# Mamba-2 SSD and a SwiGLU feed-forward on one core: four products with decays moved to GpSimd, and a new order up to the first products of block 1

## The chip, the core and the metric

The kernel runs on one core of one Trainium2 chip. The core has five engines with an instruction queue each: TensorE (PE in the profile, with its weight loads shown as PEld), VectorE (DVE), ScalarE (ACT), GpSimd (POOL) and SyncE (SP), which here only issues DMAs. The metric is the time of one execution on the device in microseconds (us).

## The reference

A state-space layer (4 batches, 8 heads, 768 tokens, head size 32, state size 16), then an RMS norm and a SwiGLU feed-forward layer over the 3072 tokens (model size 256, hidden size 1536), all in float32:

```python
log_a = np.log(np.clip(a, 1e-06, 1.0))
for c in range(nc):                                   # chunks of the sequence
    cum = np.cumsum(la, axis=-1)
    L = np.exp(cum[:, :, :, None] - cum[:, :, None, :]) * causal
    CB = np.einsum('bhin,bhjn->bhij', Cc, Bc)
    y_intra = np.einsum('bhij,bhjd->bhid', CB * L, xc)
    decay_to_i = np.exp(cum)
    y_inter = np.einsum('bhin,bhnd->bhid', Cc, state) * decay_to_i[:, :, :, None]
    y[:, :, sl] = y_intra + y_inter
    decay_from_j = np.exp(cum[:, :, -1:] - cum)
    Bx = np.einsum('bhjn,bhjd->bhjnd', Bc, xc) * decay_from_j[:, :, :, None, None]
    state = np.exp(np.sum(la, axis=-1))[:, :, None, None] * state + np.sum(Bx, axis=2)
x = y.transpose(0, 2, 1, 3).reshape(B * S, H * D)
xn = x / np.sqrt(np.mean(x * x, axis=-1, keepdims=True) + 1e-06) * rms_g
g, val = xn @ w_gate, xn @ w_val
out = (g * (1.0 / (1.0 + np.exp(-g))) * val) @ w_out
```

## The kernel before

**The work.** Tokens go in six blocks of 512 (0 to 5). The state-space layer goes by chunks of 128 tokens in twelve pairs p (two pairs to a block); from pair 2 on each chunk is cut in halves of 64. For one pair: the decays L (`mask`, `sums`, `exp` in pairs 0 and 1; `spread`, `sub`, `ex` later), C and B times their decays (`scale`, L512, instruction L518: Cd = C times `to_i` in pairs 0 and 1 alone, Bd = B times `from_j` in all pairs), transposes of B and C (`turn`, `T`, `Tt`; of Cd: `last`, `Tl`), products CB (`g`, or `gg` for a pair at once, L576 and L583), L times CB (`L`, `L1`), the additions to the state (`A`) and the states (`S`, L670), and the outputs (`y`). ScalarE then takes y out (`yt`) and squares it (`sq`), PE means the squares (`ms`), ScalarE takes the roots (`rs`, a logarithm and an exponential), and VectorE normalizes (`xn`, L831).

**The weights** come in 18 pieces of integer words (`fetch.k`, a DMA that SyncE issues) and are rebuilt: `pow.k` on ScalarE, `man.k` and `wt.k` on VectorE (L216 and L219, L225). Pieces 0 to 11 are gate and value weights, 128 columns in pieces 0 and 1 and 256 in the following pairs of pieces; 12 to 17 are output weights.

**The feed-forward layer of block 0** is done by plain products for the first 768 hidden columns (`early.0`, `early.1`, `gate.2` to `gate.5`, each followed by `silu` and `hid`). All other products of gate and value weights use a Strassen-like scheme by groups j of 256 hidden columns: PE's `P.k.j` (L935; each is four 128x256 products), ScalarE's `take.k.j` (copies a bank, L941), VectorE's sums `C.c.j` (L947), `silug`/`silu` on ScalarE, and `hidg` on VectorE or `hidgp` on GpSimd (L960). It needs combinations of weights (`cw.j.k` on VectorE, `cwp.j.k` on GpSimd, L904) and of the normalized x (`tx.b.k`, `txp.b.k`, L912). Block 0's output products are `o.0` to `o.11` (L967).

**The order.** Everything is issued by one string of some 1600 steps, written out in the kernel, `block:step.arguments/bank`. Two tables (`first_kinds` for steps with the prefix `0:`, `kinds` for the rest) give each step its function, and the engine with it. Each engine, and SyncE's DMA queue, runs its own instructions in the order of the string, and waits at an instruction until what it reads is written and its buffer or PSUM bank is free. Of these buffers two matter below: c, the sums, has four (`bufs=4`); the banks of `P` have two for gate and two for val. So moving a step past steps of other engines changes nothing by itself; moving it past steps of its own engine changes what its engine does first.

Of the kernel before, what the change touches and what calls it, by code (L numbers as in the profile page):

```python
# [9 lines left out]
FP32 = mybir.dt.float32  # L10
# [5 lines left out]
ALU = mybir.AluOpType  # L16
# [4 lines left out]
def kernel(  # L21
# [42 lines left out]
    T = NB * S  # L64
# [447 lines left out]
    def scale(p):  # L512
        s = st[p]
        b, c0 = divmod(2 * p, NC)
        hs = slice(b * NH, (b + 1) * NH)
        for name, src, d in (("Cd", "C", to_i), ("Bd", "B", from_j))[0 if p < 2 else 1:]:
            s[name] = ssd.tile([P, 2, NH, N], FP32, tag=name, name=name)
            nc.vector.tensor_tensor(  # L518
                out=s[name], in0=s[src],
                in1=d[:, c0:c0 + 2, hs].unsqueeze(3).to_broadcast([P, 2, NH, N]), op=ALU.mult)  # L520
# [645 lines left out]
    def by_vector(out, in_, scale):  # L1166
# [10 lines left out]
        "scale": scale, "turn": turn,  # L1177
# [38 lines left out]
    def when(n, fn):  # L1216

        return lambda blk, *args: fn(blk + n, *args) if blk + n < NBLK else None

    def of_pair(n, fn):  # L1220
        return when(n, lambda b, p, *args: fn(2 * b + p, *args))

    def of_chunk(n, fn):
        return when(n, lambda b, g: fn(4 * b + g))
# [11 lines left out]
        "scale": of_pair(1, scale),  # L1236
# [12 lines left out]
        "ex": of_chunk(2, exponential), "scale2": of_pair(2, scale),  # L1249
        "table": when(2, lambda b: functions("silu")),  # L1250
# [208 lines left out]
```

## Time and profile before

| | |
|---|---|
| runs of the kernel before | 395.41, 395.79, 395.88 us; median 395.79 |
| the profiled execution | 395.41 us, its span 393.7 us |
| granted TensorE clock | 1.0 |
| HBM read / written | 22.64 / 3.74 MB |
| VectorE busy, 9–22 / 22–36 / 36–55 us | 12.25 / 13.60 / 18.48 us |
| VectorE busy, 55–70 / 70–80 / 80–95 us | 13.90 / 9.11 / 12.85 us |
| DMA engines busy, 22–36 / 36–55 / 55–70 us | 85% / 100% / 69% |

A row of an engine's timeline reads: start in us, duration in us, engine, line, operation, output and inputs by the program's names, shapes, number of instructions, and in square brackets the idle time before it with what ended that. A row of the waits reads: the waiting engine, its output and line, the engine and line that it waited for, the total in us, how often, and the longest. The first lines of the page give each engine's busy time and its share in 40 equal slices of the span (9.84 us each), in tenths.

### The profile page before, as it was taken

Reading aid. Unit: us, or ns where it says so; the run is one execution under the profiler, and the core shown is the slowest. Engines: PE = TensorE matmul, PEld = TensorE weight load, DVE = VectorE, ACT = ScalarE, POOL = GpSimd, SP = SyncE. Lnnn points to the kernel's source line nnn. Section 1 sums busy time; section 2 is a strip of 40 time slices with the busy share of each in tenths; the row PEclk is TensorE's granted clock in tenths of the full one; section 3 lists DMA queues with packets and bytes.
Section 4 is the critical chain, followed back from the end, with each engine's and each line's share of the span. In section 5 each row is a group of like instructions: output and inputs, shape, how many; then the busy total and the mean of one; then the engine's idle time right before and its main releaser. Section 6 shows DMA issues by size and latency. Waiting matters only on the chain.

```text
span 393.7 us, 9631 instructions
## 1 busy us (share of the span) xinstructions
PE 386.9 (98%) x3837; PEld 332.2 (84%) x3837; DVE 285.3 (72%) x594; ACT 234.1 (59%) x483; POOL 151.8 (39%) x170
## 2 busy tenths in 40 slices
PE   8999999999999999999999999999999999999996
PEld 5675478888888899888889888899888899988995
DVE  7999999997748967484897765676654587455574
ACT  3899889978599492447651544676345740555410
POOL 5022054454648378003563611466402155211271
PEclk9999999999999999999999999999999999999999
DMA  8988986682002538202423002000100000100001
GB/s 93 252 173 249 246 153 210 121 160 63 6 0 68 78 85 128 70 0 36 102 44 75 15 0 68 2 23 28 43 0 3 0 8 27 55 0 2 1 2 53
DMA packets 92533, 27.01 MB, mean 69 GB/s; under 512 B 77416, under 2 KB 86344, under 8 KB 92488
## 3 DMA queue, kind: packets, MB, share of 16 engines
q1 hardware_dynamic: 90408, 26.26, 29.8%
q8 instruction: 30, 0.49, 0.5%
q10 hardware_dynamic: 2080, 0.13, 0.4%
q14 instruction: 15, 0.12, 0.1%
HBM read 22.64 MB, written 3.74 MB: 67 GB/s over the span
## 4 chain that ended last, share of the span: by engine, by line
PE 81%; DVE 11%; issue 4%; ACT 3%; DVEq 0%; ACTq 0%
PE gate L935 27%; PE o L1056 21%; PE val L935 20%; PE o L967 4%; PE y L720 3%; PE g L583 1%; DVE wgv L225 1%; DVE m L219 1%; DVE m L216 1%; PE tp L533 1%; DVE hid L882 1%; PE g L576 1%; PE e L453 1%; PE y L648 1%; DVE S L672 1%
## 5 line engine op out<-in xcount | busy, mean ns | idle before, releaser
L947 DVE TENSOR_TENSOR c<-val,p 128x512 f32<-128x512 f32 x99 | 67.5, 687 | 40.3 <-PE val L935 28.3
L941 ACT COPY p<-gate 128x512 f32<-128x512 f32 x99 | 56.9, 584 | 58.0 <-PE gate L935 56.3
L960 POOL TENSOR_TENSOR hid<-c 128x256 f32<-128x256 f32 x41 | 34.0, 837 | 88.8 <-ACT c L197 82.6
L935 PE MATMUL gate<-tx,wgv 128*128 128x256 f32 x264 | 65.8, 382 | 0.0
L197 ACT ACTIVATE c<-c 128x256 f32<-128x256 f32 x99 | 39.3, 415 | 30.1 <-DVE c L947 29.6
L935 PEld LDWEIGHTS gate<-tx,wgv 128*128 128x128 f32 x264 | 49.0, 190 | 7.2 <-issue 0.3
L960 DVE TENSOR_TENSOR hid<-c 128x256 f32<-128x256 f32 x58 | 28.4, 498 | 17.0 <-ACT c L197 17.0
L1087 DVE TENSOR_TENSOR ob<-ob,o 128x128 f32<-128x128 f32 (+1 forms) x90 | 24.4, 299 | 20.7 <-PE o L1056 18.0
L1056 PE MATMUL o<-two,hid 128*128 128x128 f32 x280 | 36.2, 276 | 0.1
L1056 PEld LDWEIGHTS o<-two,hid 128*128 128x128 f32 x280 | 34.4, 192 | 1.1 <-issue 0.2
L935 PE MATMUL val<-tx,sw 128*128 128x256 f32 x132 | 34.0, 382 | 0.0
L935 PE MATMUL val<-xn,sw 128*128 128x256 f32 x132 | 33.7, 380 | 0.0
L935 PE MATMUL gate<-tx,sw 128*128 128x256 f32 x132 | 33.4, 381 | 0.0
L935 PE MATMUL gate<-xn,wgv 128*128 128x256 f32 x132 | 33.2, 381 | 0.2 <-DVE xn L831 0.2
L935 PE MATMUL val<-xn,wgv 128*128 128x256 f32 x132 | 33.3, 380 | 0.0
L486 POOL TENSOR_SCALAR_AFFINE_SELECT L<-L 64x512 f32<-64x512 f32 x32 | 23.0, 718 | 13.5 <-ACT L L197 10.9
L935 PEld LDWEIGHTS val<-tx,sw 128*128 128x128 f32 x132 | 24.7, 190 | 4.0 <-issue 0.4
L935 PEld LDWEIGHTS val<-xn,wgv 128*128 128x128 f32 x132 | 24.9, 190 | 3.4
L935 PEld LDWEIGHTS gate<-xn,wgv 128*128 128x128 f32 x132 | 24.4, 190 | 4.0 <-ACT e L197 0.6
L935 PEld LDWEIGHTS gate<-tx,sw 128*128 128x128 f32 x132 | 24.6, 190 | 3.4 <-issue 0.2
L197 ACT ACTIVATE u<-gate 128x256 f32<-128x256 f32 (+1 forms) x37 | 14.8, 402 | 21.2 <-PE gate L935 20.1
L935 PEld LDWEIGHTS val<-xn,sw 128*128 128x128 f32 x132 | 24.5, 190 | 3.2 <-issue 0.2
(199 smaller groups left out, 737.2 us busy)
## 6 DMA issues: line engine op xcount, KB each, us to landing
L<-rowd SPq DMA_DIRECT2D x32, 128.0 KB, 3.3
xr<-in_x_dram SPq DMA_DIRECT2D x24, 128.0 KB, 3.8
wr<-in_moe_w_out_dram SPq DMA_DIRECT2D x6, 512.0 KB, 3.6
out_dram<-ob SPq DMA_DIRECT2D x24, 128.0 KB, 1.7
wr<-in_moe_w_gate_dram SPq DMA_DIRECT2D x5, 512.0 KB, 6.3
wr<-in_moe_w_val_dram SPq DMA_DIRECT2D x5, 512.0 KB, 4.9
br<-in_B_dram SPq DMA_DIRECT2D x23, 64.0 KB, 2.9
cr<-in_C_dram SPq DMA_DIRECT2D x23, 64.0 KB, 2.9
```

The lines of the kernel that those rows point to most:

```text
L197: nc.scalar.activation(**operands)
L216: nc.vector.tensor_scalar(out=m, in0=hi, scalar1=0xFFFFF, scalar2=0x100000, op0=ALU.bitwise_and, op1=ALU.bitwise_or)
L219: nc.vector.scalar_tensor_tensor(out=f, in0=lo.bitcast(U32), scalar=2.0 ** -32, in1=m, op0=ALU.mult, op1=ALU.add)
L486: nc.gpsimd.affine_select(out=L[r], in_=L[r], pattern=[[0, L.shape[1]], [1, HC]], compare_op=ALU.is_ge, fill=0.0, base=0, channel_multipli ...
L720: nc.tensor.matmul(out=y[2 * k + u][rows, (2 * n + i) * HC:(2 * n + i + 1) * HC], start=(k, u, rows.start) not in opened, stop=True, skip_ ...
L935: nc.tensor.matmul(out=dst[:, half[w]], lhsT=lhsT, rhs=rhs, start=(k in (1, 2, 5) and w == 0), stop=True, skip_group_check=True)
L941: nc.scalar.copy(out=t, in_=Xs[j])
L947: nc.vector.tensor_tensor(out=t, in0=Zs[j], in1=a, op=ALU.add)
L960: engine.tensor_tensor(out=hid[:, 2 * j + c // 10 - 1, c % 10 - 1], in0=u, in1=src[:, half[1]], op=ALU.mult)
L967: nc.tensor.matmul(out=o, lhsT=hid[:, f, k // 2, (k % 2) * P:(k % 2 + 1) * P], rhs=wo[:, f], start=opens, stop=(f == NF - 1), skip_group_c ...
L1056: nc.tensor.matmul(out=Os[blk, b][:, place * P:(place + 1) * P], lhsT=hidden_or_sum(u)[:, g], rhs=rhs, start=(blk, b) not in opened, stop= ...
L1087: nc.vector.tensor_tensor(out=o, in0=o, in1=src, op=ALU.add if what[0] == "+" else ALU.subtract)
```

## The change

`scale` does one product a call (k = 0 for Cd, 1 for Bd) and takes the engine as an argument; a new step `scalep` calls it with GpSimd. The steps `0:scale.1` and `0:scale.0`, two VectorE products each, become `0:scalep.1.0`, `0:scalep.1.1`, `0:scalep.0.0` and `0:scalep.0.1` on GpSimd. Of pair 5 the product moves to GpSimd as well. (`scale2p` is defined and not used in the new stretch.)

Of the string, the part from `0:fetch.7` to `1:P.6.0` is in a new order. In it some further steps change their engine. From VectorE to GpSimd go `cw.0.1`, `cw.1.2`, `cw.3.1`, `cw.4.0`, `tx.1.0`, `tx.1.3`, `1:cw.2.0` and `cw.1.1`; from GpSimd to VectorE go `cwp.1.0`, `cwp.4.3`, `cwp.5.3` and `hidgp.11.3`, `hidgp.22.4`, `hidgp.12.3`. Among the other moves: `fetch.7` to behind `dT.2`; `pow.11` from ahead of `P.1.3` to behind `P.7.3`; `P.4.5` from behind `o.1` to ahead of it; `silug.22.4`, `silug.22.3`, `silug.12.3` and `silug.21.4` to ahead of `take.7.5`; `hidgp.11.5` to behind the GpSimd steps `txp.1.0`, `txp.1.1`, `1:cwp.2.0` and `cwp.0.1`; `man.17` to behind `1:C.11.1`. The lists of products and of DMAs are the same.

```diff
@@ -509,15 +509,15 @@
         subtract(g)
         exponential(g)
 
-    def scale(p):
+    def scale(p, k=1, engine=nc.vector):
         s = st[p]
         b, c0 = divmod(2 * p, NC)
         hs = slice(b * NH, (b + 1) * NH)
-        for name, src, d in (("Cd", "C", to_i), ("Bd", "B", from_j))[0 if p < 2 else 1:]:
-            s[name] = ssd.tile([P, 2, NH, N], FP32, tag=name, name=name)
-            nc.vector.tensor_tensor(
-                out=s[name], in0=s[src],
-                in1=d[:, c0:c0 + 2, hs].unsqueeze(3).to_broadcast([P, 2, NH, N]), op=ALU.mult)
+        name, src, d = (("Cd", "C", to_i), ("Bd", "B", from_j))[k]
+        s[name] = ssd.tile([P, 2, NH, N], FP32, tag=name, name=name)
+        engine.tensor_tensor(
+            out=s[name], in0=s[src],
+            in1=d[:, c0:c0 + 2, hs].unsqueeze(3).to_broadcast([P, 2, NH, N]), op=ALU.mult)
 
     def transposed(p):
         s = st[p]
@@ -1174,7 +1174,7 @@
         "r": sums_of_logs, "parts": three_parts,
         "d": other_sums, "dx": other_decays,
         "c": chunk_sums, "cx": chunk_decays, "cc": chunk_column,
-        "scale": scale, "turn": turn,
+        "scale": scale, "scalep": lambda p, k=1: scale(p, k, pl), "turn": turn,
         "T": lambda p: turned(p, ac.copy if p else dv.tensor_copy),
         "Tt": lambda p, t: turned_of(p, by_scalar, t), "Tb": turned_of_both,
         "dT": spread_decays, "Td": turned_decayed,
@@ -1233,7 +1233,7 @@
         "turn": of_pair(1, turn), "T": of_pair(1, lambda p: turned(p, ac.copy)),
         "Tt": of_pair(1, lambda p, t: turned_of(p, by_scalar, t)),
         "dT": of_pair(1, spread_decays), "Td": of_pair(1, turned_decayed),
-        "scale": of_pair(1, scale),
+        "scale": of_pair(1, scale), "scalep": of_pair(1, lambda p: scale(p, 1, pl)),
         "g": when(1, lambda b: products_of_block(b, pair_of_banks("g", 2))),
         "L": when(1, decayed_block), "L1": when(1, decayed_block),
         "A": of_pair(1, additions), "S": of_pair(1, states),
@@ -1247,6 +1247,7 @@
         "bc": of_pair(2, load), "x": of_pair(2, load_x), "spread": of_chunk(2, spread), "sub": of_chunk(2, subtract),
         "subp": of_chunk(2, lambda g: subtract(g, nc.gpsimd)),
         "ex": of_chunk(2, exponential), "scale2": of_pair(2, scale),
+        "scale2p": of_pair(2, lambda p: scale(p, 1, pl)),
         "table": when(2, lambda b: functions("silu")),
         "exps": when(1, lambda b: functions("exp")),
     }
@@ -1256,37 +1257,37 @@
         0:part 0:hmask 0:upto 0:mid 0:mids 0:part2 0:aT 0:mask.1.1/2 0:la0 0:log4.0.4 0:upto2 0:r.0
         0:fetch.2 0:head 0:sel 0:middles 0:after2 0:fetch.3 0:log4.4.2 0:log4.6.2 0:bc.3 0:tmask
         0:parts.0 0:log 0:c*2 0:cx 0:mask.0.1/1 0:turn.0 0:Tb.0 0:T.0 0:d 0:dx 0:sums.0.1 0:sums.0.0
-        0:exp.0.1 0:never16 1:exps 0:exp.0.0 0:turn.1 0:scale.1 0:last.1 0:cc 0:scale.0 0:T.1 0:mean
-        0:g.0.1/1 0:Tt.1.0 0:g.0.0/0 0:Tt.1.1 0:L.0.1 0:L.0.0 0:sums.1.1 0:exp.1.1 0:row.1
-        0:rowout.1 0:man.0 0:bc.2 0:mask.1.0/1 0:sums.1.0 0:rowe.1 0:g.1.1/0 0:L.1.1 0:Tl.1
-        0:g.1.0/2 0:exp.1.0 0:L.1.0 0:fetch.4 0:last.0 0:Tl.0 0:fetch.7 0:dT.2 0:tok 0:tokout 0:A.1
-        0:A.0 0:S.0 0:S.1 0:pow.0 0:wt.0 0:y.0/1 0:sq.0 0:pow.1 0:y.1/2 0:sq.1 0:row.0 0:yt.0
-        0:man.1 0:wt.1 0:mask.3/1 0:rowe.0 0:yt.1 0:ydone.1 0:r.1 0:man.3 0:scale.3 0:eps
-        0:early.0.0/0 0:early.0.1 0:rowout.0 0:ms.0 0:parts.1 0:pow.3 0:pow.2 0:wt.3 0:rs.0
-        0:mask.2/2 0:scale.2 0:man.2 0:wt.2 0:sums.3 0:sums.2 0:exp.3 0:turn.2 0:T.2 0:Tt.2.0 0:xn.0
-        0:turn.3 0:norm.0 0:T.3 0:Tt.3.1 0:Tt.2.1 0:fetch.5 0:Tt.3.0 0:exp.2 0:Td.2 0:early.1.0/1
-        0:early.1.1 0:dT.3 0:man.4 0:table.1 0:x.2 0:norm.1 0:man.5 0:Td.3 0:silu.0 0:hid.0 0:pow.4
-        0:gate.2/0 0:txp.0.0 0:cw.0.0 0:gg.2/1 0:L.2.0 0:wt.4 0:man.7 0:pow.5 0:wt.5 0:L1.2.2
-        0:fetch.8 0:fetch.9 0:silu.2 0:hid.2 0:man.8 0:pow.8 0:wt.8 0:L1.2.3 0:gate.3/2 0:pow.7
-        0:gate.4/1 0:fetch.6 0:man.6 0:A.2 0:txp.0.1 0:silu.3 0:x.3 0:table.0 0:hid.3 0:pow.6
-        0:gate.5/0 0:tx.0.2 1:dT.0 1:table 0:txp.0.3 0:fetch.11 0:wt.7 0:man.9 0:fetch.10 0:S.2
-        0:silu.4 0:pow.9 0:fetch.12 0:hid.4 0:bc.5 0:wt.6 0:cwp.3.0 0:wt.9 0:silu.5 0:hid.5 0:man.11
-        0:cw.3.1 0:cw.3.2 0:cw.4.0 0:fetch.13 0:silu.1 0:y.2/2 0:S.3 0:x.5 0:cwp.4.1 0:ydone.0
-        0:switch.1 0:P.2.3 0:bc.4 0:x.4 0:switch.0 0:pow.11 0:P.1.3 0:P.1.4 0:take.1.3 0:C.11.3
-        0:P.2.4 0:P.6.3 0:yt.2 0:sq.2 0:gg.3/2 0:take.1.4 0:silug.11.3 0:C.11.4 0:L.3.0 0:take.6.3
-        0:cwp.3.3 0:P.5.3 1:spread.0 0:cwp.1.0 0:P.7.3 0:silug.11.4 0:P.6.4 0:take.7.3 0:P.5.4
-        0:P.4.3 0:hidgp.11.3 1:dT.1 0:wt.11 0:L1.3.2 0:scale.5 0:L1.3.3 0:cwp.4.2 0:cwp.4.3
-        0:take.6.4 0:C.22.3 0:P.3.3 0:man.10 0:scale.4 0:pow.10 0:wt.10 0:silug.21.3 0:cwp.5.0
-        0:cwp.5.1 0:hidg.11.4 0:P.7.4 0:take.7.4 0:y.3/2 0:C.12.3 0:hidg.21.3 0:fetch.15 1:S.0 1:S.1
-        0:P.1.5 0:P.2.5 0:pow.12 0:P.4.4 0:take.1.5 0:C.11.5 0:cw.1.2 0:P.6.5 0:C.22.4 0:fetch.14
-        0:sq.3 0:cwp.5.2 0:yt.3 0:spread.10 1:spread.1 0:man.12 0:take.6.5 0:ms.1 0:P.5.5
-        0:spread.11 0:rs.1 1:turn.1 0:wt.12 0:silug.22.3 0:hidgp.22.3 0:hid.1 0:cwp.5.3 0:P.7.5
-        0:o.0/2 0:P.3.4 0:take.7.5 0:man.15 0:silug.12.3 0:cw.1.1 0:hidgp.12.3 0:silug.21.4 0:man.13
-        0:o.1 0:P.4.5 0:C.22.5 0:hidg.21.4 0:pow.13 0:wt.13 0:P.3.5 0:C.12.4 0:silug.22.4
-        0:hidgp.22.4 0:man.14 0:silug.21.5 0:silug.22.5 0:silug.11.5 0:C.12.5 0:pow.14 0:hidg.21.5
-        0:fetch.17 0:pow.15 0:o.2 0:cw.0.1 0:rb.1 0:o.3 0:xn.1 1:P.1.0 0:silug.12.5 0:wt.14
-        0:hidgp.11.5 0:man.17 1:bc.0 1:take.1.0 1:P.1.1 0:tx.1.0 1:P.2.1 1:T.1 0:txp.1.1 0:o.4
-        0:tx.1.2 1:take.1.1 1:P.6.1 0:pow.17 1:cw.2.0 0:hidgp.22.5 0:tx.1.3 1:C.11.1 1:silu.11.1
+        0:exp.0.1 0:never16 1:exps 0:exp.0.0 0:turn.1 0:scalep.1.0 0:scalep.1.1 0:last.1 0:cc
+        0:scalep.0.0 0:scalep.0.1 0:T.1 0:mean 0:g.0.1/1 0:Tt.1.0 0:g.0.0/0 0:Tt.1.1 0:L.0.1 0:L.0.0
+        0:sums.1.1 0:exp.1.1 0:row.1 0:rowout.1 0:man.0 0:bc.2 0:mask.1.0/1 0:sums.1.0 0:rowe.1
+        0:g.1.1/0 0:L.1.1 0:Tl.1 0:g.1.0/2 0:exp.1.0 0:L.1.0 0:fetch.4 0:last.0 0:Tl.0 0:dT.2 0:tok
+        0:tokout 0:A.1 0:A.0 0:S.0 0:S.1 0:pow.0 0:fetch.7 0:wt.0 0:y.0/1 0:sq.0 0:pow.1 0:y.1/2
+        0:sq.1 0:row.0 0:yt.0 0:man.1 0:wt.1 0:mask.3/1 0:rowe.0 0:yt.1 0:ydone.1 0:r.1 0:man.3
+        0:scale.3 0:eps 0:early.0.0/0 0:early.0.1 0:rowout.0 0:ms.0 0:parts.1 0:pow.3 0:pow.2 0:wt.3
+        0:rs.0 0:mask.2/2 0:scale.2 0:man.2 0:wt.2 0:sums.3 0:sums.2 0:exp.3 0:turn.2 0:T.2 0:Tt.2.0
+        0:xn.0 0:turn.3 0:norm.0 0:T.3 0:Tt.3.1 0:Tt.2.1 0:fetch.5 0:Tt.3.0 0:exp.2 0:Td.2
+        0:early.1.0/1 0:early.1.1 0:dT.3 0:man.4 0:table.1 0:x.2 0:norm.1 0:man.5 0:Td.3 0:silu.0
+        0:hid.0 0:pow.4 0:txp.0.0 0:txp.0.1 0:silu.1 0:wt.4 0:fetch.6 0:ydone.0 0:gate.3/2 0:gg.2/1
+        0:pow.5 0:cw.1.0 0:L.2.0 0:silu.3 0:fetch.11 0:L1.2.3 0:fetch.9 0:pow.6 0:L1.2.2 0:man.6
+        0:wt.5 0:hid.3 0:man.7 0:cwp.1.1 0:gate.2/0 0:A.2 0:silu.2 0:hid.2 0:gate.4/1 0:pow.7
+        0:fetch.8 0:S.2 0:wt.6 0:wt.7 0:gate.5/0 0:x.3 0:pow.9 0:man.8 0:silu.4 0:hid.4 0:pow.8
+        0:man.9 0:wt.9 0:cwp.3.0 0:silu.5 0:y.2/2 0:cw.3.2 0:hid.5 0:wt.8 0:cwp.3.1 0:cwp.4.0
+        0:switch.1 0:P.2.3 0:switch.0 0:tx.0.2 0:S.3 0:bc.4 0:man.11 0:yt.2 0:P.1.3 0:take.1.3
+        0:fetch.10 0:P.1.4 0:C.11.3 0:sq.2 0:P.2.4 0:scale.4 0:take.1.4 0:C.11.4 0:txp.0.3 0:P.6.3
+        0:gg.3/2 0:L1.3.2 0:P.5.3 0:take.6.3 0:P.7.3 0:pow.11 0:cwp.4.1 0:silug.11.3 0:cwp.3.3
+        0:P.5.4 0:L1.3.3 0:hid.1 0:L.3.0 0:P.6.4 0:bc.5 0:x.4 0:take.7.3 0:C.22.3 0:man.10 0:pow.10
+        0:cwp.4.2 0:P.4.3 0:silug.21.3 0:wt.11 0:hidg.21.3 0:wt.10 0:scalep.5 0:x.5 0:hidg.11.3
+        0:P.3.3 0:C.12.3 0:y.3/2 0:cwp.5.0 0:P.1.5 1:S.0 0:take.6.4 0:P.7.4 0:fetch.12 0:pow.12
+        0:fetch.13 0:P.2.5 0:silug.11.4 0:take.1.5 0:spread.10 0:fetch.17 0:take.7.4 0:cwp.5.1
+        0:P.6.5 0:P.4.4 0:fetch.14 1:S.1 0:sq.3 0:C.22.4 0:yt.3 0:man.12 0:take.6.5 0:fetch.15
+        0:cw.4.3 0:cwp.5.2 0:spread.11 1:turn.1 0:ms.1 0:P.7.5 0:hidg.11.4 0:rs.1 0:silug.22.4
+        0:C.11.5 0:cw.0.0 0:wt.12 0:silug.22.3 0:hidgp.22.3 0:P.3.4 0:P.5.5 0:silug.12.3 0:man.14
+        0:o.0/2 0:silug.21.4 0:take.7.5 0:C.22.5 0:hidg.21.4 0:man.13 0:P.4.5 0:o.1 0:pow.13
+        0:cw.5.3 0:wt.13 0:man.15 0:hidg.22.4 0:P.3.5 0:o.2 0:silug.21.5 0:hidg.21.5 0:o.3 1:table
+        0:pow.14 1:dT.0 0:wt.14 0:rb.1 0:cwp.1.2 0:xn.1 0:silug.22.5 0:C.12.4 0:hidgp.22.5 0:txp.1.0
+        1:spread.0 0:txp.1.1 0:hidg.12.3 0:silug.11.5 0:pow.15 1:P.1.1 1:take.1.1 0:C.12.5 1:cwp.2.0
+        0:tx.1.2 1:P.2.1 1:spread.1 1:C.11.1 0:cwp.0.1 0:silug.12.5 1:P.1.0 0:pow.17 1:P.6.1
+        0:table.0 0:o.4 1:dT.1 1:take.1.0 0:hidgp.11.5 1:bc.0 0:man.17 0:txp.1.3 1:T.1 1:silu.11.1
         1:P.6.0 1:sub.0 1:P.2.0 0:wt.15 0:wt.17 1:turn.0 1:C.11.0 0:cwp.0.2 1:Tt.1.0 1:hid.11.1
         1:take.6.0 1:P.7.0 1:take.7.0 1:take.6.1 1:silu.11.0 1:P.5.1 1:P.5.0 1:P.4.0 1:C.22.0
         0:cwp.0.3 0:fetch.16 1:silu.21.0 0:spread.9 1:P.7.1 1:P.3.0 1:cwp.2.2 1:hid.21.0 0:ydone.3
```

## The prediction

> **What bounds the kernel now.** I read the page first, then what TensorE (PE) waits for, then each engine's timeline where the steps differ (about 9.5 to 92 us).
>
> ```profile
> PE 386.9 (98%) x3837; PEld 332.2 (84%) x3837; DVE 285.3 (72%) x594; ACT 234.1 (59%) x483; POOL 151.8 (39%) x170
> ...
> PE   8999999999999999999999999999999999999996
> ...
> DVE  7999999997748967484897765676654587455574
> ```
>
> PE is busy in nearly every slice, VectorE (DVE) only until about 95 us. The page's first two parts say that time is PE's work plus the few places where PE has nothing to do. The change leaves PE's list of products as it was and only moves them. So it can gain no more than PE's idle places inside the reordered stretch, and it loses whatever new ones it makes. What PE waits for, over the whole span:
>
> ```profile
> PE idle L322 <- DVE warm L348: 1.1, 1, 1.1
> PE o L1056 <- DVE ob L1087: 0.9, 2, 0.5
> PE y L689 <- DVE S L670: 0.5, 1, 0.5
> PE g L583 <- ACT sq L197: 0.5, 1, 0.5
> PE gate L935 <- DVE xn L831: 0.2, 1, 0.2
> ```
>
> Only the last three lie after 9.5 us and before the old order resumes. Measured from start to start they are a little longer. Eight 128x256 products take 1.73 us (two groups of PE's timeline start at 88.25 and 89.98), 0.216 each; P.6.3 begins at 53.54, so gg.3 could begin at 54.40 and begins at 55.08: 0.68 us lost. o.2 and o.3 begin at 76.14, 16 products end at 79.60, block 1 begins at 79.97: 0.37 lost. **The ceiling of the gain is thus 0.68 + 0.37 = 1.05 us**; the wait for S.0 at 18.40 hangs on a chain that the first edit does not shorten (next paragraph).
>
> **The four steps on GpSimd.** On VectorE the products with the decays stand so:
>
> ```profile
> 9.50 0.43 DVE L518 TENSOR_TENSOR Cd<-cr,d_sb 128x256 f32<-128x256 f32 x1
> 9.84 0.42 DVE L518 TENSOR_TENSOR Bd<-br,d_sb 128x256 f32<-128x256 f32 x1
> ...
> 11.90 2.36 DVE L622 TENSOR_TENSOR L<-g,L 128x1024 f32<-128x1024 f32 x2 [0.33 <-PE g L576]
> ```
>
> Four of them free 4 x 0.34 = 1.36 us of VectorE (start to start), worth nothing: VectorE then already waits 0.33 us for PE's g, so it only waits longer. What can be lost is the other end: PE's transposes of Cd (last.1, 10.34) now wait for GpSimd. It is free from 9.03 (its 128x416 product starts at 7.97 and takes 1.06) and starts when d_sb is there, at 9.50. No row shows this product on GpSimd; a 128x256 product of two SBUF operands takes 0.73 alone (30.85) and up to 1.25 (85.23). Cd is ready at 10.23 to 10.75, the two transposes issue in 0.22, and g.0.1 starts at 10.65 whatever happens, since it waits for the exponential that ends at 10.54. So: nothing (with 0.73) to +0.4 us. I take 0: beside these steps VectorE runs a reduction and a memset, not work like that beside the 1.25 row. The Trainium skill (GPSIMD Engine Reference, "Elementwise — side-by-side cycle accounting") puts an elementwise product on GpSimd at 1.96 times VectorE's; that would be an estimated 0.83 us here, against 0.73 in the row, and 0 to the sum either way. Pair 1's Bd and pair 0's two end by about 12.6 (three more at 0.78) and are first read at 15.40 and 16.30: hidden, with 2.8 us to spare. Pair 5's product, which also goes to GpSimd, stands behind six others there, ends near 59.5 and is read at 62: hidden. Of the other steps that change engine between VectorE and GpSimd (combinations of weights and of x, three hidden products), VectorE is rid of seven in all; they count below where something waits for them.
>
> **The new order, 33 to 60 us.** fetch.7 goes behind dT.2 in SyncE's queue; its weights are first used 10 us after they land, and dT.3, moved back some 0.4 us, lands at 35.4 instead of 35.0, before its user at 35.97. Later x.5 waits for y.2 (about 50 us) and holds fetch.12 to fetch.15 behind it; fetch.12 then lands near 56 and is read at 61. Nothing here. VectorE's row of steps before S.3 loses man.11 (1.07, start to start), cw.3.1 and cw.4.0 (0.33 each), so S.3 starts near 51.1 instead of 52.78. ScalarE's yt.2 and sq.2 follow (2.2 us from S.3 to the end of sq.2 in the old rows: 52.78 to 55.02), and gg.3 finds its bank free at about 54.4: **-0.5 us** (0 if cwp.3.0 and cwp.3.1 slow man.8, -0.68 at best).
>
> **60 to 80 us.** ScalarE now does pow.11 (2.2) after take.6.3 instead of at 50.10, so it has no idle time left; sq.3 starts near 65.3 (65.69 before), and turn.1, which now waits for yt.3 with P.7.4 and P.4.4 already behind PE, takes back **+0.2 us** (0 to 0.75). rs.1 starts near 67.75 (68.14 before). After its two table loads of 1.28 the order puts four silu products (about 0.34 each) ahead of take.7.5, where one stood, so take.7.5 ends 5.2 us after rs.1 starts, at 73.0 (72.34 before); and P.4.5, which waits for it, now comes straight after o.0, with o.1 (1.73) no longer in front. PE is there 0.3 ahead of the old 72.69, at 72.4: **+0.65 us** (0 to 1.1). From 73.05 PE does P.4.5, o.1, P.3.5, o.2 and o.3 (0.86 + 1.73 + 0.86 + 3.46) until 79.96. VectorE does C.22.5, hidg.21.4, man.13, cw.5.3, wt.13, man.15, hidg.22.4, hidg.21.5 and wt.14 (0.60 + 0.33 + 1.07 + 0.33 + 0.62 + 1.07 + 0.33 + 0.33 + 0.62 = 5.3, from the rows' starts) until 78.3, so the first half of xn.1 (0.70) is there by 79.1 and the old wait for it goes: **-0.37 us** (0 if VectorE loses 0.9 on the way).
>
> **80 to 92 us, the step that decides.** GpSimd gets txp.1.0, cwp.2.0 and cwp.0.1 ahead of hidgp.11.5, and txp.1.3 behind it; C.11.1 on VectorE waits for hidgp.11.5 (its buffer), and behind C.11.1 stand man.17 (which ran before it), sub.0, wt.15, wt.17 and C.11.0, for which PE's P.5.0 waits. The rows there:
>
> ```profile
> 82.76 0.78 POOL L912 TENSOR_TENSOR tx<-xn,tx 128x256 f32<-128x256 f32 x1 [5.41 <-DVE tx L912]
> 83.49 0.91 POOL L960 TENSOR_TENSOR hid<-c 128x256 f32<-128x256 f32 x1
> 84.36 0.91 POOL L904 TENSOR_TENSOR wgv<-wgv 128x256 f32<-128x256 f32 x1
> 85.23 1.25 POOL L904 TENSOR_TENSOR sw<-wgv,sw 128x256 f32<-128x256 f32 x1
> ...
> 88.70 1.29 POOL L499 TENSOR_TENSOR L<-L,tok 128x512 f32<-128x512 f32 x1
> ```
>
> ```profile
> 82.86 0.95 DVE L904 TENSOR_TENSOR sw<-wgv 128x256 f32<-128x256 f32 x1
> ...
> 84.61 0.68 DVE L947 TENSOR_TENSOR c<-val,p 128x512 f32<-128x512 f32 x1
> 85.21 0.68 DVE L499 TENSOR_TENSOR L<-L,tok 128x512 f32<-128x512 f32 x1
> 85.81 2.35 DVE L225 SCALAR_TENSOR_TENSOR wo<-m,e 128x512 f32<-128x512 f32 x2
> 88.08 0.68 DVE L947 TENSOR_TENSOR c<-val,p 128x512 f32<-128x512 f32 x1
> ```
>
> The six GpSimd products from 82.76 to 88.70 take 0.99 us each from start to start. Five of them (txp.1.0, txp.1.1, cwp.2.0, cwp.0.1, hidgp.11.5) after xn.1's first half end at 84.1 if that ends at 79.1, at 84.8 if it ends at 79.78 as in the old rows; I take the later, since GpSimd also blocks xn.1 itself (last rival); C.11.1 starts at 84.9. From C.11.1 to C.11.0 the rows give 84.61 to 88.08 = 3.47; man.17 adds 1.07 (81.12 to 82.19); C.11.0 itself takes 0.68. Ready at 90.1. PE is at P.5.0 at 89.11 less 0.02 (the sum so far): a stall of about **+1.1 us**. Bounds: 0.70 per product (3.5 for five, the spacing of GpSimd alone at 55.10 to 56.48) and xn.1 0.7 earlier make C.11.0 ready at 88.0 and cost nothing; man.17 beside GpSimd (+0.41, L219 at 1.10 against 0.69) makes 1.5. I take 1.1 since the spacing of 0.99 is from this very stretch. Behind it the order is the old one and PE has no slack to give the time back.
>
> **Sum.** 0 - 0.5 + 0.2 + 0.65 - 0.37 + 1.1 = +1.1. The profiled execution took 395.41 us (span 393.7 and 1.7 around it), so 396.5 for one like it; the median of the three runs is 395.79, 0.38 higher, so **396.9** against that.
>
> **Rivals.**
> *No change (395.8).* The gain at gg.3 and the new wait at P.4.5 cancel (-0.02, with xn.1) and GpSimd runs at its uncontended 0.70, so C.11.0 is in time. For it: each step moved is hidden by about half a microsecond. Against: the 0.99 spacing.
> *Faster (394.7).* The wait for sq.2 and that for xn.1 both go and nothing comes back: -1.05, the ceiling. It needs take.7.5 to end by 72.0 (72.69 - 0.68), so rs.1 to begin by 66.8 instead of 68.14, and C.11.1 to start by 82.8 (89.11 - 1.05 - 3.47 - 1.07 - 0.68). Against: ScalarE has no idle time left before rs.1.
> *Every pair alternates (398.0).* A VectorE instruction with both inputs in SBUF shows 0.95 beside GpSimd against 0.42 alone, 1.22 against 0.69 (the second of the L225 pair). If man.8 (+0.7: 0.29 and 0.41) beside cwp.3.0 and cwp.3.1 pays it too, the gain at gg.3 is gone, S.1 and yt.3 come 0.75 late, and C.11.0 costs 1.45: +2.2. The Trainium skill (SBUF — State Buffer, "Who interferes with whom") speaks for this rival, and against the change as a whole: the pair of ports is a lock, and a VectorE instruction with two SBUF inputs and a GpSimd instruction that reads SBUF block each other entirely. By that rule, the rows at 82.86 and 85.81 agree.
> *The change not doing what it says* is out: the program has the five L518 products on GpSimd.
>
> **Chances.** Forecast 0.45, no change 0.30, faster 0.15, every pair 0.10. Some 0.2% (0.8 us) is what a measurement of this kernel can tell. The forecast's own range runs from +0.3 to +1.9, so a sixth of it falls within 0.2%; a little of the faster case does too, and a little of the middle falls out to either side: faster 0.16, same 0.34, slower 0.50. The range for 8 in 10 goes from the ceiling of the gain, 394.7, to the lock case with 0.4 for a late Cd, 398.4.
>
> **What would show it.** In the profile after: last.1 at 10.34 to 10.5 and g.0.1 at 10.65 (right) or near 11 (0.4 lost); no PE wait for sq before gg.3; a PE wait for ScalarE's p at L935 near 72.5; VectorE idle before the first C of block 1 near 82 to 84 with GpSimd as its releaser; and PE waiting 0.7 to 1.5 us for C.11.0 near 89. If PE's list of waits shows none of the last two, the forecast is wrong and the time is 395.8 or less; if it shows over 2 us in other places, a step that I called hidden was not.

## The result

The changed kernel takes 398.08 us (median of seven runs, 396.99 to 401.57) against 395.79 (seven runs, 395.41 to 396.13): 1.0077 times the kernel before, 95% interval 1.0049 to 1.0105. By the medians that is 2.3 us more, by the ratio 3.0. Forecast were 396.9, 1.1 more. Single executions whose granted TensorE clock was 0.991 to 0.996 instead of 0.999 to 1.0 took 397.6 to 401.6 us, whatever the kernel; two of these seven (400.96 and 401.57) and one of the control's six below (401.21) are such, and without those two the median is 397.86, 2.1 more. The profiled execution took 399.11 us, 1.0 above the median; its span is 397.4 against 393.7.

The first part of the page and the list of PE's waits, after:

```profile
PE 387.8 (98%) x3837; PEld 332.2 (84%) x3837; DVE 284.1 (71%) x587; ACT 233.8 (59%) x483; POOL 156.3 (39%) x177
```

```profile
PE val L935 <- DVE c L947: 1.8, 1, 1.8
PE g L583 <- DVE T L557: 1.2, 1, 1.2
...
PE gate L935 <- ACT p L941: 0.4, 2, 0.2
```

VectorE does seven instructions less and GpSimd seven more, PE's list is as long as before. Of the three waits of before inside the reordered stretch, two are gone (gg.3 for sq, block 1 for xn). Two that were not there are larger than both together: P.5.0 (val) waits 1.8 us for a C of VectorE, and gg.2 (g) waits 1.2 us for VectorE's product with the decays, T. The third line is P.6.3 and P.4.5, which wait for ScalarE's copies.

The first of the two, in VectorE's timeline (columns as before: start, duration, engine, line, operation, tiles, and the idle time ahead of it):

```profile
85.60 0.69 DVE L947 TENSOR_TENSOR c<-val,p 128x512 f32<-128x512 f32 x1 [2.02 <-POOL hid L960]
86.21 1.02 DVE L216 TENSOR_SCALAR m<-wr 128x512 int32<-128x512 int32 x1
87.27 1.10 DVE L219 SCALAR_TENSOR_TENSOR m<-wr,m 128x512 f32<-128x512 uint32 x1
88.29 1.21 DVE L499 TENSOR_TENSOR L<-L,tok 128x512 f32<-128x512 f32 x1
89.42 2.66 DVE L225 SCALAR_TENSOR_TENSOR wo<-m,e 128x512 f32<-128x512 f32 x2
92.01 0.68 DVE L947 TENSOR_TENSOR c<-val,p 128x512 f32<-128x512 f32 x1
```

and in GpSimd's, the instructions that ran beside it:

```profile
84.83 0.73 POOL L960 TENSOR_TENSOR hid<-c 128x256 f32<-128x256 f32 x1
85.52 0.74 POOL L912 TENSOR_TENSOR tx<-xn,tx 128x256 f32<-128x256 f32 x1
86.20 0.74 POOL L904 TENSOR_TENSOR wgv<-wgv 128x256 f32<-128x256 f32 x1
86.89 0.92 POOL L904 TENSOR_TENSOR sw<-wgv,sw 128x256 f32<-128x256 f32 x1
87.78 1.18 POOL L904 TENSOR_TENSOR wgv<-wgv 128x256 f32<-128x256 f32 x1
88.91 1.18 POOL L904 TENSOR_TENSOR sw<-sw,wgv 128x256 f32<-128x256 f32 x1
```

VectorE waits 2.02 us for hidgp.11.5 (the first GpSimd row) and then does C.11.1, man.17 (two rows), sub.0, wt.15 with wt.17, and C.11.0, which PE needs for P.5.0. From C.11.1 to C.11.0 it takes 92.01 - 85.60 = 6.41 us. man.17 alone takes 88.29 - 86.21 = 2.08, and took 82.19 - 81.12 = 1.07 in the kernel before, where GpSimd was idle beside it:

```profile
81.12 0.43 DVE L216 TENSOR_SCALAR m<-wr 128x512 int32<-128x512 int32 x1
81.58 0.69 DVE L219 SCALAR_TENSOR_TENSOR m<-wr,m 128x512 f32<-128x512 uint32 x1
```

The second, in VectorE's timeline near 37 us:

```profile
36.10 0.69 DVE L219 SCALAR_TENSOR_TENSOR m<-wr,m 128x512 f32<-128x512 uint32 x1
37.48 0.42 DVE L557 TENSOR_TENSOR T<-tp,dT 128x256 f32<-128x256 f32 x1 [0.68 <-DMA dT<-rowe]
```

VectorE itself waits there, for the transfer dT.3, which lands at 37.4 instead of 35.0. PE's gg.2 needs that T.

Added up, start to start on PE, the profiled executions differ so: 0.29 at g.0.1 (10.94 against 10.65, not from the change: with the same four GpSimd products in the old order it began at 10.49), 1.22 at gg.2, -0.25 inside y.2, 0.23 at P.1.3, 0.37 at P.6.3, -0.51 at gg.3, 0.09 inside y.3, 0.36 at P.4.5, -0.37 at block 1's first product, 0.19 at its second group, 1.99 at P.5.0. The sum is 3.61; P.5.0 starts at 92.74 instead of 89.11, 3.63 later, and from there both kernels run alike.

### The profile page after: what moved, and what is told of

The parts are those of the page before. It is cut to its first block, busy times and chain, and to the rows that moved or that the text cites. A ratio compares the mean times of both kernels' runs of the same rounds, so it can differ in the third digit from the quotient of the medians.

```text
span 397.4 us, 9620 instructions
## 1 busy us (share of the span) xinstructions
PE 387.8 (98%) x3837; PEld 332.2 (84%) x3837; DVE 284.1 (71%) x587; ACT 233.8 (59%) x483; POOL 156.3 (39%) x177
## 4 chain that ended last, share of the span: by engine, by line
PE 83%; ACT 8%; DVE 4%; issue 2%; DMA 2%; DVEq 0%; ACTq 0%
PE gate L935 28%; PE o L1056 21%; PE val L935 20%; PE o L967 5%; ACT e L197 3%; PE y L720 3%; PE g L583 1%; DMA wr<-in_moe_w_val_dram 1%; ACT u L197 1%; PE g L576 1%; PE e L453 1%; PE tp L533 1%; PE y L648 1%; DVE wo L225 1%; ACT sq L197 1%
## 5 line engine op out<-in xcount | busy, mean ns | idle before, releaser
L947 DVE TENSOR_TENSOR c<-val,p 128x512 f32<-128x512 f32 x99 | 67.5, 686 | 43.1 <-PE val L935 27.4
L960 POOL TENSOR_TENSOR hid<-c 128x256 f32<-128x256 f32 x38 | 31.2, 830 | 94.1 <-ACT c L197 87.3
L960 DVE TENSOR_TENSOR hid<-c 128x256 f32<-128x256 f32 x61 | 30.0, 499 | 17.0 <-ACT c L197 17.0
```

The lines of the kernel that those rows point to most:

```text
L947: nc.vector.tensor_tensor(out=t, in0=Zs[j], in1=a, op=ALU.add)
L960: engine.tensor_tensor(out=hid[:, 2 * j + c // 10 - 1, c % 10 - 1], in0=u, in1=src[:, half[1]], op=ALU.mult)
```

## The experiments

Each was timed in five rounds beside the kernel before, in three groups of four, and each ratio is to the runs of before in its own group (medians 395.67, 395.18 and 395.37 us). Across groups ratios are compared, not times.

**Control: the changed kernel again** (no edit).

> The changed kernel again. Theory 1 (two waits): its loss sits in two places, about 2 us at P.5.0 near 92 us, where PE waits for C.11.0 behind a long line on VectorE, and 0 to 1.5 us at gg.2 near 37 us, where PE waits for VectorE's Td.3 and that for the DMA dT.3, which lands at a time that differs from run to run. Median 397.3 to 398.5 against 395.8 of the kernel before; the wait at P.5.0 is there in this profile too (1.5 to 2.2 us), the one at gg.2 may be shorter or longer. Theory 2 (the four products on GpSimd upset the start): g.0.1 starts 0.3 us later than before in this profile as well.

Measured: 398.38 us (397.58 to 401.21), ratio 1.0078 (1.0053 to 1.0104). P.5.0 waits 1.8 us again, gg.2 0.6 instead of 1.2; g.0.1 starts at 10.72. VectorE's line from C.11.1 to C.11.0 takes 6.40 us again (84.33 to 90.73). Over the profiles of all these kernels g.0.1 starts between 10.25 and 11.30. So the wait at P.5.0 belongs to the kernel, the one at gg.2 to the kernel and the execution, and the 0.3 us at the start to the execution.

**man.17 ahead of C.11.1.**

```diff
-1:C.11.1 0:cwp.0.1 ... 0:hidgp.11.5 1:bc.0 0:man.17 0:txp.1.3
+0:man.17 1:C.11.1 0:cwp.0.1 ... 0:hidgp.11.5 1:bc.0 0:txp.1.3
```

> The changed kernel with one step moved: man.17 ahead of C.11.1 of block 1, into the 2.0 us in which VectorE waits for GpSimd's hidgp.11.5. By the sizes of the prediction (man.17 costs 1.1) the wait at P.5.0 falls from 2.0 to about 0.9 and the kernel gains 1.1 us. If the line is long because VectorE and GpSimd hold each other up (man.17 took 2.1 us there, sub.0 1.2 and wt.17 1.5), the gain is 1.5 to 2.0 us and the wait at P.5.0 is 0.5 at most. Rival: C.11.0 is late for another reason (wt.17's input, pow.17), then no gain.

Measured: 396.03 us (395.03 to 398.07), ratio 1.0009 (0.9993 to 1.0025). The wait at P.5.0 is gone from the list. By the medians this one step carries 2.35 us of the control's 2.7; without the control's execution of 401.21 us its median is 398.01, and the step carries 1.98, as much as the wait. Either is more than 1.1, so the line's length is not that of the rows that the prediction used. Without man.17 the line from C.11.1 to C.11.0 takes 3.49 us (85.42 to 88.91), so at its place in the changed kernel man.17 made it 2.92 longer. In this kernel man.17 still takes 0.96 + 1.10 beside GpSimd, but in time in which VectorE otherwise waited. What is left is 0.6 us at gg.2 and, new, 0.6 us at P.1.3:

```profile
PE g L583 <- DVE T L557: 0.6, 1, 0.6
PE gate L935 <- DVE hid L882: 0.6, 1, 0.6
```

**hidgp.11.5 at the head of GpSimd's line.**

```diff
-1:cwp.2.0 0:tx.1.2 ... 0:cwp.0.1 ... 1:take.1.0 0:hidgp.11.5 1:bc.0
+0:hidgp.11.5 1:cwp.2.0 0:tx.1.2 ... 0:cwp.0.1 ... 1:take.1.0 1:bc.0
```

> The changed kernel with one step moved: hidgp.11.5 to the head of GpSimd's line, ahead of cwp.2.0 of block 1. C.11.1 on VectorE then need not wait 2.0 us for it. If only the length of the line counts, no gain; if, as the prediction has it, its late start counts as well, C.11.1 starts 1.5 to 2.0 us earlier and the wait at P.5.0 falls from 2.0 to 0.5 or less: 1.5 to 2.0 us faster than the changed kernel, about the same as with man.17 moved.

Measured: 395.20 us (394.70 to 398.54), ratio 1.0001 (0.9985 to 1.0016). VectorE's timeline:

```profile
82.38 0.69 DVE L947 TENSOR_TENSOR c<-val,p 128x512 f32<-128x512 f32 x1 [0.62 <-POOL hid L960]
82.99 0.42 DVE L216 TENSOR_SCALAR m<-wr 128x512 int32<-128x512 int32 x1
...
87.88 0.68 DVE L947 TENSOR_TENSOR c<-val,p 128x512 f32<-128x512 f32 x1
```

The wait ahead of C.11.1 falls from 2.02 to 0.62, the line is 5.50 long, and PE no longer waits at P.5.0. By the ratios (1.0001 against the control's 1.0078) it gains 3.0 us, by the medians without the control's 401.21 us 2.5 (each against the kernel before in its own group), more than the 1.5 to 2.0 expected; in its profile the other waits are small too (gg.2 0.2, P.1.3 none), and why is not separated here. So start and length of the line count alike: taking either away is enough.

**GpSimd's work beside the line taken away.** VectorE's instructions and their order are unchanged.

```diff
-0:cwp.0.2 ... 1:cwp.2.2
-0:txp.1.3 ... 0:cwp.0.3 ... 1:cwp.2.1      # subtractions and sums on GpSimd
+0:txd.1.3 ... 0:cwd.0.3 ... 1:cwd.2.1      # dma_start(out=..., in_=one operand)
-0:subp.9 1:twop.2
+1:twop.2 0:subp.9
```

> The changed kernel without GpSimd's work beside VectorE's line from C.11.1 to C.11.0: of the five products that follow hidgp.11.5 there, cwp.0.2 and cwp.2.2 of block 1 are left out (their weights stay uncombined), txp.1.3, cwp.0.3 and cwp.2.1 are replaced by DMA copies of one operand, and subp.9 stands behind twop.2. VectorE's own steps and their order are those of the changed kernel. If the line is long because the two engines hold each other up: man.17 takes 1.1 (2.1 with GpSimd busy), sub.0 0.7 (1.2), wt.15 and wt.17 1.3 to 2.4 together (2.7), C.11.0 comes 4.5 us after C.11.1 instead of 6.4, and the wait at P.5.0 falls from 2.0 to 0.2 or nothing: 1.8 to 2.1 us faster than the changed kernel (398.1 to 398.4). If the operations are long for another reason (transfers into the same memory, the data), the rows and the wait stay.

Measured: 394.96 us (394.52 to 395.65), ratio 0.9987 (0.9978 to 0.9995). VectorE's timeline:

```profile
83.80 0.69 DVE L953 TENSOR_TENSOR c<-val,p 128x512 f32<-128x512 f32 x1 [2.00 <-POOL hid L966]
84.41 0.42 DVE L216 TENSOR_SCALAR m<-wr 128x512 int32<-128x512 int32 x1
84.86 0.69 DVE L219 SCALAR_TENSOR_TENSOR m<-wr,m 128x512 f32<-128x512 uint32 x1
85.47 0.68 DVE L499 TENSOR_TENSOR L<-L,tok 128x512 f32<-128x512 f32 x1
86.07 1.29 DVE L225 SCALAR_TENSOR_TENSOR wo<-m,e 128x512 f32<-128x512 f32 x2
87.28 0.68 DVE L953 TENSOR_TENSOR c<-val,p 128x512 f32<-128x512 f32 x1
```

(L953 and L966 here are L947 and L960 of the other kernels.) VectorE still waits 2.00 us for hidgp.11.5, and the same instructions then take 87.28 - 83.80 = 3.48 us instead of 6.41. Every one of them but the C is shorter: 1.02 to 0.42, 1.10 to 0.69, 1.21 to 0.68, 2.66 to 1.29. PE does not wait at P.5.0, whose turn comes at 88.96 here: C.11.0 ends at 87.96, and with 2.93 us more it would end at 90.89, 1.93 late, which is the wait of the changed kernel. This is the cause shown: GpSimd's products beside it add 2.93 us to a line of VectorE's that would have been in time. By the ratios the gain over the control is 3.6 us, by the medians without the control's 401.21 us 2.75, again more than the wait of 2.0; what the rest is, this experiment does not separate. Its time is no version's, since work is missing.

**gate.2 ahead of gg.2.**

```diff
-0:gate.3/2 0:gg.2/1 ... 0:cwp.1.1 0:gate.2/0 0:A.2
+0:gate.3/2 0:gate.2/0 0:gg.2/1 ... 0:cwp.1.1 0:A.2
```

> The changed kernel with one step moved: gate.2 ahead of gg.2, so that PE has 3.5 us of products in front of gg.2. Theory 1: the wait of gg.2 for Td.3 is gone, a gain as large as that wait is in the other runs of the changed kernel (0.5 to 1.2 us), and the wait at P.5.0 stays (1.5 to 2.2). Rival: the later L.2.0, A.2 and S.2 bring a new wait at y.2, no gain.

Measured: 399.17 us (398.99 to 399.81), ratio 1.0093 (1.0077 to 1.0109), against the control's 1.0078: no gain, and by the medians 0.8 us slower still, though the intervals overlap. The wait of gg.2 is gone, and A.2 waits 1.1 us for VectorE's L1 steps (L628), which now come behind the later gg.2, P.1.3 1.0 us for hid.5. The rival was right in kind. The stretch from 37 to 52 us hangs on several lines at once, and covering one wait with PE's own work uncovers the next.

**silu.5 ahead of pow.8, hid.5 ahead of wt.9**, on top of man.17.

```diff
-0:silu.4 0:hid.4 0:pow.8 0:man.9 0:wt.9 0:cwp.3.0 0:silu.5 0:y.2/2 0:cw.3.2 0:hid.5 0:wt.8
+0:silu.4 0:hid.4 0:silu.5 0:pow.8 0:man.9 0:hid.5 0:wt.9 0:cwp.3.0 0:y.2/2 0:cw.3.2 0:wt.8
```

> The changed kernel with man.17 ahead of C.11.1 and, besides, silu.5 ahead of pow.8 on ScalarE and hid.5 ahead of wt.9 on VectorE. Theory: the new order holds PE up at P.1.3 near 51 us (0.2 to 0.7 us), because hid.5, which gives P.1.3 its bank, waits for silu.5 and that stands behind pow.8 (2.2 us). With silu.5 in front the wait goes: 0.3 to 0.7 us faster than with man.17 alone (396.0), about 395.5. Rival: wt.8 or S.3 become late in its place and PE waits at P.1.4 or gg.3, no gain.

Measured: 396.18 us (395.43 to 401.51), ratio 1.0025 (1.0006 to 1.0044), against 1.0009 with man.17 alone: no gain. hid.5 is out of the list of waits, so that was the right owner; in its place PE waits 0.31 at P.1.4, which starts at 52.1, where wt.8, now 0.55 late for pow.8, ends; and 0.63 instead of 0.37 at P.6.3. The rival again.

**fetch.7 back ahead of dT.2**, on top of man.17, and **fetch.7's move alone in the kernel before.**

```diff
-0:fetch.4 0:last.0 0:Tl.0 0:dT.2 ... 0:pow.0 0:fetch.7 0:wt.0      # the changed order
+0:fetch.4 0:last.0 0:Tl.0 0:fetch.7 0:dT.2 ... 0:pow.0 0:wt.0      # the order before
```

> The changed kernel with man.17 ahead of C.11.1 and, besides, fetch.7 back ahead of dT.2 in SyncE's queue. The prediction held that place to cost nothing. Theory: fetch.7 behind dT.2 delays rowe.0, which is issued behind it, and so dT.3, Td.3 and gg.2 by about 0.5 us or more; with fetch.7 back, the wait of gg.2 for Td.3 shrinks by 0.5 or goes, but what PE gains there it partly waits again at P.1.3 for hid.5, since that line on ScalarE and VectorE does not hang on gg.2: the time changes by -0.5 to 0 against man.17 alone (396.0). Rival: dT.3 lands late for a reason that lies ahead of it in the queue (how fast the DMA engines take the loads before it), no change of the wait at gg.2.

> The kernel before with one DMA moved: fetch.7 from ahead of dT.2 to behind pow.0, as the changed order has it. The prediction put this at nothing (dT.3 some 0.4 us later, still before its user). Theory now: SyncE's queue runs 0.3 to 1.5 us later in some executions than in the one that the prediction was read from, so 0.5 us more is not hidden: dT.3 is issued 4.9 to 5.2 us after dT.2 (4.5 to 5.0 without the move), PE waits 0.2 to 0.8 us at gg.2, and the time is 0.2 to 0.5 us above the kernel before. Rival: hidden, no change.

Measured: with fetch.7 back 395.26 us (394.91 to 397.91), ratio 1.0005 (0.9990 to 1.0019), against 1.0009 without; fetch.7 moved in the kernel before 395.56 (395.06 to 396.11), ratio 1.0006 (0.9997 to 1.0015). Neither time is apart from no change. The traces say a little more. SyncE issues rowe.0 0.75 us after dT.2 with fetch.7 in front and 1.25 after it with fetch.7 between them. dT.3 waits for rowe.0 to land. dT.3's issue stands 4.06 us ahead of gg.2's first product with fetch.7 back, and 2.13 to 3.48 ahead in seven profiles with the changed place (gate.2's experiment apart, where gg.2 comes later). PE waits for T in five of those seven 0.2 to 1.2 us, and 0.1 in the other two. With fetch.7 in front it does not wait in two changed orders, but there gg.2's first product itself came late (36.63 and 36.50, against 35.57 to 36.27 in the seven). It waits 0.8 us in a third changed order with fetch.7 in front (the first way of the last experiment, lead 2.62), and 0.4 in the old order with the four products on GpSimd (lead 3.60). In the kernel before, with fetch.7 moved, the lead was 3.47 and gg.2 did not wait. So the move takes some 0.5 us of slack; the wait at gg.2 comes with and without it, and that the move costs time by itself is not shown.

**The four products alone**: on GpSimd in the old order, and back on VectorE in the new.

```diff
-0:scale.1 0:last.1 0:cc 0:scale.0                                     # the old order
+0:scalep.1.0 0:scalep.1.1 0:last.1 0:cc 0:scalep.0.0 0:scalep.0.1
```

> The kernel before, in its old order, with only the four products of pairs 0 and 1 moved to GpSimd. By the prediction's first term: no change (within 0.3 us), Cd about 0.6 to 0.7 each on GpSimd, and g.0.1 straight behind the exponential. Rival: the four products cost 0.3 us or more at g.0.1, or help by as much as VectorE is freed (up to 1.4 us).

> The changed kernel with the four products of pairs 0 and 1 back on VectorE, the new order kept. Theory 1: no change against the changed kernel (within 0.3 us), both waits are there. Theory 2 (the four products on GpSimd delay the start by 0.3 us and with it the line of DMAs in front of dT.3): 0.3 to 1.5 us faster than the changed kernel, g.0.1 back at 10.65, and the wait at gg.2 gone.

Measured: on GpSimd in the old order 395.96 us (395.23 to 396.76), ratio 1.0014 (1.0004 to 1.0025), 0.55 us slower (0.16 to 0.99). Back on VectorE in the new order 397.97 (397.71 to 398.27), ratio 1.0061 (1.0047 to 1.0074) against the control's 1.0078, intervals overlapping: 0.4 us faster by the medians, and 0.04 without the control's execution of 401.21 us. So a cost of the four products is not shown there; in its profile P.5.0 waits 1.8 as before, gg.2 0.1 instead of 0.6 and P.1.3 0.3. GpSimd's timeline in the old order:

```profile
9.39 0.62 POOL L518 TENSOR_TENSOR Cd<-cr,d_sb 128x256 f32<-128x256 f32 x1 [0.51 <-ACT d_sb L197]
9.97 0.62 POOL L518 TENSOR_TENSOR Bd<-br,d_sb 128x256 f32<-128x256 f32 x1
```

Cd takes 0.62, is ready at 10.01, and last.1 and g.0.1 start at 10.18 and 10.49, 1.13 after the exponential starts as in the kernel before (9.51 to 10.65). So at the place where the prediction looked for a cost there is none, and still the kernel is a little slower. In this profile gg.2 waits 0.4 us for T, which it did not before. Here the late transfer was the one before dT.3: VectorE waits for dT.2 and does the T of dT.3, which had landed at 35.50, without a wait of its own at 36.22:

```profile
32.44 0.42 DVE L557 TENSOR_TENSOR T<-tp,dT 128x256 f32<-128x256 f32 x1 [0.62 <-DMA dT<-rowe]
36.22 0.41 DVE L557 TENSOR_TENSOR T<-tp,dT 128x256 f32<-128x256 f32 x1
```

Over all profiles (gate.2's apart) gg.2 waits 0.1 us at most in the four with the products on VectorE, and 0.1 to 1.2 in eight of the nine with them on GpSimd. With one profile of each kernel that is a hint and no proof. How four products at 10 us would bring a transfer at 32 us late is not shown: SyncE issues rowe.1 17.4 to 18.3 us after its first load of x in ten profiles with the products on GpSimd, and 16.9 to 18.0 after it in four with them on VectorE, ranges that overlap. This stays open.

**All of it mended**, in two ways.

```diff
+0:man.17 1:C.11.1                                    # first way: man.17, and
+0:silu.4 0:hid.4 0:silu.5 0:pow.8 0:man.9 0:hid.5    # silu.5 and hid.5, and
+0:fetch.7 0:dT.2                                     # fetch.7 ahead of dT.2, and
+0:o.1 0:P.4.5                                        # P.4.5 behind o.1
```

> The changed kernel with five steps moved: man.17 ahead of C.11.1; silu.5 ahead of pow.8 and hid.5 ahead of wt.9; fetch.7 behind rowe.0; o.1 back ahead of P.4.5. Each removes one wait of PE that the changed order made (P.5.0 2.0, P.1.3 0.2 to 0.7, gg.2 0 to 1.2, P.4.5 0.36). If they add, what is left is the gain of the new order, no wait of gg.3 for sq.2 (0.68, less 0.37 at P.6.3) and none for xn.1 (0.37, less 0.19 at P.2.1): 395.1 to 395.5, 0.2 to 0.6 us faster than the kernel before. Rival: a new wait comes for each removed, 395.8 or more.

Measured: 396.21 us (395.27 to 398.12), ratio 1.0021 (1.0006 to 1.0035). The kernel that ran has fetch.7 ahead of dT.2, as in the order before, and not behind rowe.0; either way nothing stands between dT.2 and rowe.0. The rival came true: P.4.5 no longer waits, but P.3.5 0.30 behind it, P.6.3 loses 0.64 instead of 0.37, and 0.4 come up at block 1's second group; gg.2 waits 0.8, with VectorE waiting 0.77 for dT.2 and 0.28 for dT.3.

```diff
+0:man.17 1:C.11.1                                    # second way: man.17, and
+0:fetch.7 0:dT.2                                     # fetch.7 back, and
+0:scale.1.0 0:scale.1.1 ... 0:scale.0.0 0:scale.0.1  # the four products on VectorE
```

> The changed kernel with man.17 ahead of C.11.1, fetch.7 back ahead of dT.2, and the four products of pairs 0 and 1 back on VectorE. With man.17 and fetch.7 alone the ratio to the kernel before was 1.0005. If the four products cost 0.4 to 0.55 us (as the two comparisons of them alone suggest), this comes out at 0.9990 to 0.9995 of the kernel before, 0.2 to 0.4 us faster. Rival: with fetch.7 in front there is slack at gg.2 and the four products cost nothing: the ratio stays 1.0005.

Measured: 394.97 us (394.64 to 396.07) against 395.37, ratio 0.9990 (0.9982 to 0.9999). It is ahead of both kernels, by 0.4 us (0.04 to 0.7) on the kernel before. Against 1.0005 with the products on GpSimd that is 0.6 us by the ratios, but the two intervals overlap. Of the three comparisons, only the one in the old order shows by itself that the four products cost time.

## Why the prediction was wrong

Its direction, its place and its mechanism at P.5.0 were right. Its size was not: 1.1 us forecast, 2.3 by the medians. The small terms agreed by luck: their sum was put at -0.02 and came as +0.11 in the profiled execution (all places but g.0.1, gg.2 and P.5.0), while most of them were off and the errors cancelled.

**P.5.0, the term that decided, was mis-sized: 1.1 forecast (bounds 0 to 1.5), 2.0 measured.** (The prediction's own figures make 84.9 + 3.47 + 1.07 + 0.68 - 89.09 = 1.03.) The step that failed is the length of VectorE's line from C.11.1 to C.11.0, put at 3.47 + 1.07 = 4.54 us and measured at 6.41. The 1.07 for man.17 came from rows beside which GpSimd was idle; at its new place GpSimd had five products in a row. man.17 took 2.08, sub.0 1.13 instead of 0.60, wt.15 and wt.17 2.59 instead of 2.27. The bound above, 0.41 more for L219 alone, was too low: L216, which has one input in SBUF, went from 0.43 to 1.02 as well, and I had counted only instructions with two. The start of the line was misjudged the other way: C.11.1 began 5.15 us ahead of P.5.0's turn (85.60 against 90.75), forecast were 4.19. GpSimd's five products up to hidgp.11.5 took 4.42 us (81.14 to 85.56) and not 5 times 0.99, its last ones 0.68 apart while VectorE waited. A line 1.87 longer less a start 0.96 earlier is the 0.9 by which the term was low.

The Trainium skill (SBUF — State Buffer, "Who interferes with whom") has the rule that I used for two SBUF inputs, and in the same list says that a tensor_scalar in its two-port mode also takes the shared ports. The traces agree with both: L216, a tensor_scalar, took 1.02 in this line with GpSimd busy and 0.42 with it idle (in which mode it ran, no trace tells; with hidgp.11.5 moved it took 0.42 at 82.99 although GpSimd was busy), while the C instructions, with one input in PSUM, stay at 0.68 to 0.69 in all of them. The fourth rival was built on that rule and gave 398.0, close to what came, in part by luck: of its three places C.11.0 took part, and man.8 with 0.41 (its L219 at 47.74 took 1.10 beside cwp.3.0); turn.1, behind yt.3, did not wait, and the rest of the loss was at gg.2, which the rival did not have.

**"Nothing here" at fetch.7 failed in the trace.** The lead of dT.3 was read from one execution (35.0 against a user at 35.97) and the move put at 0.4 us. In the profiled execution of the changed kernel dT.3 landed 2.4 later. It was issued 2.47 later (34.14 against 31.67): 1.40 because SyncE's queue up to dT.2, whose list of transfers the change leaves as it was, ran late (rowe.1 issued at 25.20 against 23.73), 0.50 for fetch.7 between dT.2 and rowe.0, and 0.57 because rowe.0, for which dT.3 waits, took longer. PE's gg.2 waited 1.22 in that execution and 0 to 0.8 in others.

**The gain at gg.3, -0.5, came as -0.16 and was used up.** gg.3 did not wait for sq.2 (0.51 gained there, and 0.25 in y.2), but P.6.3 just ahead of it lost 0.37 for ScalarE's copies and P.1.3 0.23 for hid.5. S.3 did not start at 51.1 but at 53.15. 1.51 of that is VectorE's own late start behind the T of dT.3 (37.48 against 35.97); besides, VectorE waited 0.29 for a weight at 40.99, and man.8's L219 took 0.41 more beside cwp.3.0, which the prediction had named as what would undo this gain. I had moved S.3 by the VectorE steps that left, and not followed what VectorE would wait for in the rest.

**The small terms.** turn.1: +0.2 forecast, 0 measured. P.4.5: +0.65 forecast, 0.36 measured (take.7.5 ended at 74.35). The wait for xn.1: gone as forecast (-0.37), with 0.19 back one group later. The four products: 0 at g.0.1 as forecast, and 0.55 (0.16 to 0.99) in the time of the old order by a way that was not found.

Of the signs named beforehand, VectorE's idle time ahead of block 1's first C with GpSimd as its releaser is there (2.02), and so is PE's wait for C.11.0 (1.8, outside the 0.7 to 1.5). A wait of over 1 us at gg.2 was named nowhere.

## What to carry to other kernels

When a step is moved, take its duration from rows that have the same neighbours on the other engine, not from the place that it leaves: here a line of six VectorE instructions was 3.48 us with GpSimd idle and 6.41 with it busy. A wait on another engine costs least when the steps that do not depend on it stand in front: one step moved into VectorE's 2 us of waiting returned some 2 us. A lead of a transfer that was read from one execution is worth no more than the spread of that queue from run to run, and one profile of each kernel does not explain a wait behind it.

## What the runs showed of the hardware

Beside GpSimd products, VectorE's 128x512 instructions from SBUF took 1.02 instead of 0.42 (L216, a tensor_scalar with one input), 1.10 instead of 0.69 (L219), 1.21 instead of 0.68 (L499), 2.66 instead of 1.29 for two (L225); a sum with an input in PSUM (L947) was 0.68 to 0.69 in either case. In the fourteen profiles together, L219 took 1.10 to 1.12 in all 40 cases in which a GpSimd instruction ran beside it, each time with some 0.56 us of that instruction left, and 0.69 to 0.70 in the other 212. The others are less regular beside GpSimd: L216 took 0.42 to 1.02, L499 0.68 to 1.22; what decides that was not tested. GpSimd's product with decays took 0.62 where VectorE's took 0.43. SyncE's queue, with the same transfers ahead, issued rowe.1 between 23.73 and 25.20 us over fourteen profiles.
